# High and low value parts from one matmul of 129 columns, in the last 24 of 32 attention pairs

## The chip, the cores and the metric

The kernel runs on one core of a Trainium2 chip. The metric is the device time of one execution in microseconds. Engines are named as in the profile: PE multiplies matrices, PEld is its weight load, DVE is the vector engine, ACT the scalar engine, POOL the GpSimd engine, SP issues DMA transfers. Before the change the kernel took 1162.68 us (median of three runs, 1161.75 to 1164.28).

## The reference

Attention over pooled queries, and behind it a gated unit over the attention's output. What the change touches is the last product of the attention, `attn @ v`, and its division by the row sums:

```python
def _attn_ref(q, k, v):                       # 8 batches, 8 heads, 1152 keys, 64 dims
    q_pool = q.reshape(B, H, S // 2, 2, D).mean(axis=3)          # 576 queries
    scores = scale * np.matmul(q_pool, k.transpose(0, 1, 3, 2))
    scores = scores - np.max(scores, axis=-1, keepdims=True)
    attn = np.exp(scores)
    attn = attn / (np.sum(attn, axis=-1, keepdims=True) + 1e-09)
    return np.matmul(attn, v)

def _moe_ref(x, w_in, w_spatial, b_spatial, w_out):              # x: attention output, 8 x 576 x 512
    h = np.maximum(x @ w_in, 0.0)
    u, v = h[..., :512], h[..., 512:]
    v_n = (v - mean(v)) / np.sqrt(var(v) + 1e-06)
    v_s = np.einsum('ts,bsd->btd', w_spatial, v_n) + b_spatial[None, :, None]
    return (u * v_s) @ w_out
```

## The kernel before

The 64 heads are worked in 32 pairs (`i` from 0 to 31). Every fp32 factor is held as two 16-bit parts, a high one and a low one, and a product is the sum of the matmuls of its parts. For a pair, `attention(i)` goes through 18 steps, nine key chunks of 128 for each of the two heads. A step makes a 128x512 tile of transposed scores in a bank `pss` (two matmuls, L1081 and L1082), ACT writes its exponential to the tile `pt` (L1087), and POOL takes the rest of `pt` apart in place (L1107): `top` is the upper half of each fp32 word read as bf16, `rst` the remainder as fp16. The last 64 queries of a head are worked apart, in `ptl` and `tail_values` (L1051 to L1053).

Two steps later `values(i, k)` multiplies the step's `pt` with the chunk's values. The values lie in `vp` as 130 columns a chunk: 0 to 63 the low part, 64 to 127 the high part, 128 a column of ones, 129 unused. The 512 queries are four blocks of 128, and each block has 65 columns in the bank `o`: 64 of output, and one that collects the row sums from the ones. A step has twelve matmuls in three rounds over the four blocks: `top` with high part and ones (65 columns, L977), `top` with the low part onto the first 64 of the same columns (L983), `rst` with high part and ones (65 columns, L988). In the first eight pairs (`i < EARLY`) three of the nine chunks go through whole fp32 matmuls instead (L970).

There is one bank `o` (`ps_o` with one buffer). It is full after a head's ninth chunk. Then DVE adds a small constant to the four row sums and takes the reciprocal (L949 and L950, `den`) and multiplies the four blocks into the tile `xm` (L996), and the next head's first matmul may write the bank. `turn()` puts off a head's first value step by one step more, so that other work lies between two heads. After a pair's second head `xm` is turned over, from the ninth pair on through ACT, POOL and a transposing DMA (L1006, L1007).

Beside these steps run, as generators advanced at set rates: `maxima` of the next pair (matmuls L869 and L854 of 384 columns into `pm`, DVE maxima L875), `prep` of the pair after that, the values of the next pair, and from the ninth pair on the gated unit of the two batches that are finished (L1168, L1235, L1279, L1280, L1322, with `vv<-u,gs,vv` at L496 on DVE).

The order on the engines isn't the order of the code. `Order.pin` collects all instructions with their dependencies, gives each a cost by size and engine, goes twice through a list schedule (forward, then a backward pass that ranks by time to the end, then forward again), and pins the order that comes out on every engine. A different instruction, or another cost, can so change the order of everything after it.

Of the kernel before, what the change touches and what calls it, by code (L numbers as in the profile page):

```python
# [17 lines left out]
AF = mybir.ActivationFunctionType  # L18
ALU = mybir.AluOpType
# [356 lines left out]
def attn_sgu_kernel(ctx: ExitStack, tc: tile.TileContext, qT, kT, v, w_in, w_spT, b_sp, w_out, out):  # L376
    nc = tc.nc
    P = 128
    B, NHP, _, D, _, S = qT.shape
    NC = kT.shape[4]  # L380
# [17 lines left out]
    WHOLE = (1, 4, 7)  # L398
    EARLY = 2 * NHP
    MOE_RATE = 0.5  # L400
    D1 = D + 1
    VW = 2 * D + 2
# [262 lines left out]
    whole = {}  # L665
# [280 lines left out]
    def inverse(src, name):  # L946

        r = sm.tile(list(src.shape), F32, name=name, bufs=2)
        nc.vector.tensor_scalar_add(r, src, 1e-9 * PEXP)  # L949
        nc.vector.reciprocal(r, r)  # L950
        return r
# [4 lines left out]
    def values(i, k):  # L956


        st = state[i]
        h, c = divmod(k, NC)  # L960
        if c == 0:
            st["o"] = ps_o.tile([P, MAIN], F32, name="o")
        o = st["o"][:, : 4 * D1].rearrange("p (t d) -> p t d", d=D1)
        pt = st["pt"][k]
        top = pt.bitcast(BF16)[:, 1::2]
        rst = pt.bitcast(F16)[:, 0::2]
        vp = vps[i % 2][:, h, c]
        if i < EARLY and c in WHOLE:
            for t in range(4):
                nc.tensor.matmul(  # L970
                    o[:, t], lhsT=pt[:, t * P : (t + 1) * P], rhs=whole[i][:, h, WHOLE.index(c)],
                    start=False, stop=False, skip_group_check=True,
                )
            return
        for t in range(4):
            cols = slice(t * P, (t + 1) * P)
            nc.tensor.matmul(  # L977
                o[:, t], lhsT=top[:, cols], rhs=vp[:, D : D + D1], start=c == 0 and t == 0, stop=False,
                skip_group_check=True,
            )  # L980
        for t in range(4):
            cols = slice(t * P, (t + 1) * P)
            nc.tensor.matmul(  # L983
                o[:, t, 0:D], lhsT=top[:, cols], rhs=vp[:, 0:D], start=False, stop=False, skip_group_check=True
            )
        for t in range(4):
            cols = slice(t * P, (t + 1) * P)
            nc.tensor.matmul(  # L988
                o[:, t], lhsT=rst[:, cols], rhs=vp[:, D : D + D1], start=False, stop=c == NC - 1,
                skip_group_check=True,  # L990
            )
        if c == NC - 1:
            if h == 0:
                st["xm"] = wk.tile([P, 4, P], F32, name="xm", bufs=1)
            r = inverse(o[:, :, D], "den")
            nc.vector.tensor_tensor(  # L996
                out=st["xm"][:, :, h * D : (h + 1) * D], in0=o[:, :, 0:D],
                in1=r.unsqueeze(2).to_broadcast([P, 4, D]), op=ALU.mult,
            )
            if h == 1:  # L1000
                later.append([2, lambda: turn_main(i)])
# [12 lines left out]
    def turn_main(i):  # L1014

        b, hp = divmod(i, NHP)
        n, e = divmod(b, 2)
        xm = state.pop(i)["xm"]
        if i < EARLY:
            ps = ps_m.tile([P, 512], F32, name="pm")  # L1020
            for t in range(4):
                nc.tensor.transpose(out=ps[:, t * P : (t + 1) * P], in_=xm[:, t], identity=ident)
            x_split(x_rows(n, e)[:, :, hp], ps)
        else:
            turn_by_dma(xm, n, e, hp)
        if hp == NHP - 1:
            xc = wk.tile([P, 2, NHP, P], F16, name="xc", bufs=1)
            nc.scalar.activation(xc[:, 0], xt, AF.Copy, bias=0.0, scale=1.0)
            nc.gpsimd.tensor_sub(xc[:, 1], xt, xc[:, 0])
            ps = ps_m.tile([P, 512], F32, name="pm")  # L1030
            for k in range(2 * NHP):
                nc.tensor.matmul(
                    ps[:, k * TAIL : (k + 1) * TAIL], lhsT=xc[:, k // NHP, k % NHP], rhs=ident2, start=True, stop=True
                )
            nc.scalar.activation(
                x_rows(n, None)[:, :, :, e * TAIL : (e + 1) * TAIL],
                ps.rearrange("p (l k t) -> p l k t", l=2, t=TAIL), AF.Copy, bias=0.0, scale=1.0,
            )
            if ends_unit(i):
                units.append(gated_unit(n))  # L1040
# [18 lines left out]
    def turn(last=False):  # L1059

        while todo and (last or len(todo) > LAG):
            if not last and todo[0][1] % NC == 0 and len(todo) <= LAG + 1:
                break
            values(*todo.popleft())
        for x in list(later):
            x[0] -= 1
            if x[0] <= 0 or last:
                later.remove(x)
                x[1]()
# [420 lines left out]
```

## Time and profile before

| | |
|---|---|
| timed runs | 1162.68 us median (1161.75 to 1164.28) |
| profiled execution | a span of 1164.0 us from first to last instruction; it has no time of its own beside the runs |
| granted TensorE clock | 0.996 on average |
| instructions in the profile | 33534 |
| matmuls | 13297, each with a weight load |
| value matmuls at L977, L983, L988 | 2112 each, 193 ns mean length of one |
| DMA | 133.18 MB in 89146 packets |

The page is read by asking first which engine is short of time, then in which stage. A matmul's length (193 ns here) is from its start until its result has landed; the next one starts long before that, so what a matmul takes of PE is the distance from its start to the next start. The profile shows two stages with attention: the first eight pairs, up to about 250 us, with loads, weights and little else for PE to turn to, and the remaining 24 pairs together with the gated units, up to about 1064 us. Behind them comes the last gated unit alone.

```profile
PE   4989999999999999999999999999999999999998
DVE  7799999977889987865778757874778757742644
ACT  6788889997879978778877878878787876844433
POOL 3667766888998988879887888978878888974000
```

These are the busy tenths in 40 slices of 29.1 us: PE is at 9 from the third slice on, while the three others keep some room.

### The profile page before, as it was taken

The page shows a single profiled execution, that of the slowest core. Times are in us where ns is not written, and L with a number is a line of the kernel's source. Part 1 is how long each engine was busy: PE and PEld are TensorE (multiplying, and loading weights), DVE is VectorE, ACT ScalarE, POOL GpSimd, SP SyncE. Part 2 cuts the span into 40 slices and gives each one's busy share as a digit, 9 for nine tenths or more (in the row PEclk, how much of TensorE's full clock was granted, in tenths as well). Part 3 has the DMA queues.
Part 4 walks back from the last instruction along what each step waited for, and adds up shares of the span by engine and source line. Part 5 has one row for each costly group of instructions (what it writes and reads, how often), then busy time and mean ns, then how long its engine had stood idle before and what let it go on. Part 6 is the DMA issues. An engine that isn't in the chain of part 4 may idle for free.

```text
span 1164.0 us, 33534 instructions
## 1 busy us (share of the span) xinstructions
PE 1131.7 (97%) x13297; PEld 718.2 (62%) x13297; DVE 870.9 (75%) x2239; ACT 892.4 (77%) x1697; POOL 860.6 (74%) x739
## 2 busy tenths in 40 slices
PE   4989999999999999999999999999999999999998
PEld 1667777766666665665666666566666666665453
DVE  7799999977889987865778757874778757742644
ACT  6788889997879978778877878878787876844433
POOL 3667766888998988879887888978878888974000
PEclk9989999999999999999999999999999999999999
DMA  6666455444553354454433444355533412221002
GB/s 208 185 206 168 131 167 179 122 123 123 137 144 83 77 139 109 142 143 125 125 96 83 145 120 110 99 133 159 144 92 99 128 34 68 47 63 37 1 1 82
DMA packets 89146, 133.18 MB, mean 114 GB/s; under 512 B 39902, under 2 KB 48158, under 8 KB 88988
## 3 DMA queue, kind: packets, MB, share of 16 engines
q1 hardware_dynamic: 88988, 131.04, 40.4%
q8 instruction: 104, 1.70, 0.6%
q14 instruction: 54, 0.44, 0.1%
HBM read 81.20 MB, written 9.44 MB: 78 GB/s over the span
## 4 chain that ended last, share of the span: by engine, by line
PE 85%; DVE 8%; ACT 3%; DMA 2%; issue 1%; SPq 0%; POOL 0%; ACTq 0%; DVEq 0%; POOLq 0%
PE pss L1081 9%; PE pss L1082 9%; PE pm L869 8%; PE pw L1279 7%; PE pw L1235 6%; PE pw L1168 6%; PE pw L1322 6%; PE o L977 5%; PE o L988 5%; PE o L983 5%; DVE mt L875 3%; PE o L970 3%; PE pm L1051 1%; PE pss L1168 1%; PE pm L1053 1%; PE pm L1052 1%
## 5 line engine op out<-in xcount | busy, mean ns | idle before, releaser
L1107 POOL TENSOR_TENSOR pt<-pt 128x512 f16<-128x512 f32 x528 | 579.0, 1115 | 154.1 <-ACT pt L1087 149.7
L1087 ACT ACTIVATE pt<-pss,esc 128x512 f32<-128x512 f32 x576 | 388.6, 693 | 130.0 <-PE pss L1082 115.0
L875 DVE TENSOR_REDUCE mt<-pm 128x1 f32<-128x384 f32 x733 | 385.7, 551 | 104.8 <-PE pm L869 94.2
L1081 PE MATMUL pss<-qhi,khi 128*128 128x512 f16 x576 | 219.5, 382 | 2.3 <-ACT pt L1087 2.1
L1082 PE MATMUL pss<-xq,klo 66*128 66x512 f16 (+1 forms) x576 | 219.7, 383 | 0.8 <-DMA xq<-mr 0.8
L869 PE MATMUL pm<-khi,qhi 128*128 128x384 f16 x637 | 194.0, 327 | 3.7 <-DVE mt L875 3.3
L977 PEld LDWEIGHTS <-pt 128*128 128x128 bf16 x2112 | 123.4, 98 | 60.3 <-issue 3.3
L977 PE MATMUL o<-vp,pt 128*128 128x65 f16 x2112 | 158.7, 193 | 0.3 <-DVE xm L996 0.2
L983 PE MATMUL o<-vp,pt 128*128 128x64 f16 x2112 | 157.0, 193 | 0.0
L988 PE MATMUL o<-vp,pt 128*128 128x65 f16 x2112 | 156.7, 193 | 0.0
L988 PEld LDWEIGHTS <-pt 128*128 128x128 f16 x2112 | 115.2, 98 | 36.5 <-issue 1.6
L869 PEld LDWEIGHTS <-qhi 128*128 128x128 f16 x756 | 72.9, 100 | 63.0 <-issue 11.8
L983 PEld LDWEIGHTS <-pt 128*128 128x128 bf16 x2112 | 103.6, 98 | 5.5 <-issue 0.3
L1168 PE MATMUL pw<-wi_h,xg 128*128 128x512 f16 x240 | 88.4, 379 | 0.5 <-ACT row L1342 0.5
L1235 PE MATMUL pw<-xg,wi_h 128*128 128x512 f16 (+1 forms) x336 | 82.1, 325 | 0.0
L1322 PE MATMUL pw<-wo_h,vv 128*128 128x512 f16 x216 | 78.6, 380 | 2.3 <-DVE vv L496 2.3
L1279 PE MATMUL pw<-ws_h,vv 128*128 128x512 f16 x216 | 78.2, 379 | 0.2 <-DVE u L1289 0.2
L1107 POOL TENSOR_TENSOR ptl<-ptl 128x1152 f16<-128x1152 f32 x32 | 69.8, 2181 | 9.7 <-ACT ptl L1103 9.5
L875 DVE TENSOR_REDUCE mt<-pw 128x1 f32<-128x384 f32 x131 | 69.4, 545 | 9.8 <-PE pw L869 5.1
L1103 ACT ACTIVATE ptl<-pss,esc 128x256 f32<-128x256 f32 (+1 forms) x128 | 64.6, 505 | 10.7 <-PE pss L1098 10.3
L1082 PEld LDWEIGHTS <-klo 66*128 66x128 f16 (+1 forms) x576 | 56.4, 98 | 26.0 <-issue 4.7
L1081 PEld LDWEIGHTS <-khi 128*128 128x128 f16 x576 | 56.7, 99 | 22.7 <-issue 2.6
(270 smaller groups left out, 2530.5 us busy)
## 6 DMA issues: line engine op xcount, KB each, us to landing
vt<-in_v_dram SPq DMA_DIRECT2D x56, 576.0 KB
qt<-in_qT_dram SPq DMA_DIRECT2D x32, 576.0 KB
kt<-in_kT_dram SPq DMA_DIRECT2D x32, 576.0 KB
khi<-kn SPq DMA_DIRECT2D x128, 144.0 KB
out_dram<-row SPq DMA_DIRECT2D x24, 256.0 KB
qhi<-xq SPq DMA_DIRECT2D x62, 72.0 KB
klo<-klo SPq DMA_DIRECT2D x31, 144.0 KB
u<-in_w_in_dram SPq DMA_DIRECT2D x3, 1024.0 KB
```

The source lines that it names most:

```text
L869: nc.tensor.matmul(pm[:, :W], lhsT=q[:, c0 : c0 + P], rhs=k[:, n * NB : (n + 1) * NB, :], start=True, stop=True,)
L875: nc.vector.reduce_max(out=mt[:, t, n : n + 1], in_=pm[:, :W], axis=AX.X)
L977: nc.tensor.matmul(o[:, t], lhsT=top[:, cols], rhs=vp[:, D : D + D1], start=c == 0 and t == 0, stop=False, skip_group_check=True,)
L983: nc.tensor.matmul(o[:, t, 0:D], lhsT=top[:, cols], rhs=vp[:, 0:D], start=False, stop=False, skip_group_check=True)
L988: nc.tensor.matmul(o[:, t], lhsT=rst[:, cols], rhs=vp[:, D : D + D1], start=False, stop=c == NC - 1, skip_group_check=True,)
L1081: nc.tensor.matmul(o, lhsT=khh[:, h, c, :], rhs=qhl[:, h, q], start=True, stop=False)
L1082: nc.tensor.matmul(o, lhsT=KL[0:rows, h, c, :], rhs=X[0:rows, h, q], start=False, stop=True)
L1087: nc.scalar.activation(pt, ps, AF.Exp, bias=0.0, scale=esc)
L1107: nc.gpsimd.tensor_sub(t.bitcast(F16)[..., 0::2], t, t.bitcast(BF16)[..., 1::2])
L1168: nc.tensor.matmul(ph, lhsT=rows(xa, cc, c0, c0 + P), rhs=wa[:, cc, DH:DF], start=n == 0, stop=n == 3 * NCC - 1,)
L1235: nc.tensor.matmul(pu[:, : z - a], lhsT=wa[:, cc, fc * P : (fc + 1) * P], rhs=rows(xa, cc, a, z), start=n == 0, stop=n == 3 * NCC - 1,)
L1279: nc.tensor.matmul(pv, lhsT=l, rhs=r[:, 0:MAIN], **fl)
```

## The change

From the ninth pair on (`joint = i >= EARLY`) the blocks stand 130 columns apart in the bank `o` (`pitch = VW`) in place of 65. For blocks 1 to 3, `top` is multiplied with low part, high part and ones in one matmul of 129 columns: the low part's product lands in the 64 columns ahead of the block, the rest in the block. Block 0 keeps two matmuls. The products of `rst` stay as they were. A step has nine matmuls in place of twelve, in an order written out. At the head's end ACT copies the three low products out of the bank into `xm` (L1007 of the changed kernel), DVE adds this copy to the three blocks in the bank (L1010), and then multiplies as before (L1011). The first eight pairs keep their twelve matmuls.

```diff
+        bank = st["o"]
+        joint = i >= EARLY
+        pitch = VW if joint else D1
+        def at(a, n, z=D):
+            return bass.AP(bank.tensor, bank.offset + a, [list(bank.ap[0]), [pitch, n], [1, z]])
...
+        hi, lo = slice(D, D + D1), slice(0, D)
+        def product(x, t, v, a, z):
+            nc.tensor.matmul(
+                bank[:, t * pitch + a : t * pitch + z], lhsT=x[:, part[t]], rhs=v,
+                start=c == 0 and t == 0 and x is top and z == D1, stop=x is rst and c == NC - 1, skip_group_check=True,
+            )
...
-        for t in range(4):
-            cols = slice(t * P, (t + 1) * P)
-            nc.tensor.matmul(o[:, t], lhsT=top[:, cols], rhs=vp[:, D : D + D1], ...)
-        for t in range(4):
-            cols = slice(t * P, (t + 1) * P)
-            nc.tensor.matmul(o[:, t, 0:D], lhsT=top[:, cols], rhs=vp[:, 0:D], ...)
-        for t in range(4):
-            cols = slice(t * P, (t + 1) * P)
-            nc.tensor.matmul(o[:, t], lhsT=rst[:, cols], rhs=vp[:, D : D + D1], ...)
+        if joint:
+            product(top, 0, vp[:, hi], 0, D1)
+            for t in range(1, 4):
+                product(top, t, vp[:, 0 : D + D1], -D, D1)
+            product(rst, 1, vp[:, hi], 0, D1)
+            product(rst, 2, vp[:, hi], 0, D1)
+            product(top, 0, vp[:, lo], 0, D)
+            product(rst, 3, vp[:, hi], 0, D1)
+            product(rst, 0, vp[:, hi], 0, D1)
+        else:
+            for x, v, z in ((top, hi, D1), (top, lo, D), (rst, hi, D1)):
+                for t in range(4):
+                    product(x, t, vp[:, v], 0, z)
         if c == NC - 1:
...
-            r = inverse(o[:, :, D], "den")
+            x = st["xm"][:, :, h * D : (h + 1) * D]
+            if joint:
+                nc.scalar.activation(x[:, 1:4], at(VW - D, 3), AF.Copy, bias=0.0, scale=1.0)
+            r = inverse(at(D, 4, 1)[:, :, 0], "den")
+            if joint:
+                nc.vector.tensor_add(at(VW, 3), at(VW, 3), x[:, 1:4])
             nc.vector.tensor_tensor(
-                out=st["xm"][:, :, h * D : (h + 1) * D], in0=o[:, :, 0:D],
-                in1=r.unsqueeze(2).to_broadcast([P, 4, D]), op=ALU.mult,
+                out=x, in0=at(0, 4), in1=r.unsqueeze(2).to_broadcast([P, 4, D]), op=ALU.mult
             )
```

On PE the order is the same up to the first value step of the ninth pair. There, in the middle of the step, stands before (`vp_101` is the values tile, `pt` the exponentials, the number at the end the output's columns):

```order
L977 MATMUL o<-vp_101,pt 128x65
L983 LDWEIGHTS pt
L983 MATMUL o<-vp_101,pt 128x64
L983 LDWEIGHTS pt
L983 MATMUL o<-vp_101,pt 128x64
```

And now, from the step's first joint matmul but two on:

```order
L980 MATMUL o<-vp_101,pt 128x129
L980 LDWEIGHTS pt
L980 MATMUL o<-vp_101,pt 128x65
L980 LDWEIGHTS pt
L980 MATMUL o<-vp_101,pt 128x65
L980 LDWEIGHTS pt
L980 MATMUL o<-vp_101,pt 128x64
```

Twelve loads and twelve matmuls became nine and nine; over the kernel PE has 1,296 loads and 1,296 matmuls fewer.

The second place is DVE at the end of the second head of pair 13, where the gated unit of the first two batches stands before its last product. Before:

```order
L949 TENSOR_SCALAR den<-o 128x4
L875 TENSOR_REDUCE mt<-pm 128x1 x2
L950 RECIPROCAL den<-den 128x4
L875 TENSOR_REDUCE mt<-pm 128x1
L996 TENSOR_TENSOR xm<-o,den 128x4x64
L888 TENSOR_REDUCE pm<-mt 128x4
```

And now:

```order
L949 TENSOR_SCALAR den<-o 128x4
L1071 TENSOR_SCALAR xt<-pm,dent 64x64 x2
L950 RECIPROCAL den<-den 128x4
L1010 TENSOR_TENSOR o<-o,xm 128x3x64
L1011 TENSOR_TENSOR xm<-o,den 128x4x64
L875 TENSOR_REDUCE mt<-pm 128x1 x5
```

The add stands ahead of the multiply, and the maxima that stood between moved behind both.

The third place is ACT at the same head's end. Before:

```order
L710 ACTIVATE vp_102<-vt 128x9x64
L1087 ACTIVATE pt<-pss,esc 128x512 x2
L1103 ACTIVATE ptl<-pss,esc 128x5x64
L1087 ACTIVATE pt<-pss,esc 128x512
L1103 ACTIVATE ptl<-pss,esc 128x5x64
```

And now:

```order
L709 ACTIVATE vt<-vt,vs 128x576 x2
L710 ACTIVATE vp_102<-vt 128x9x64
L1007 ACTIVATE xm<-o 128x3x64
L710 ACTIVATE vp_102<-vt 128x9x64
L1101 ACTIVATE pt<-pss,esc 128x512 x2
```

The copy stands between two parts of the next pair's values, and the exponentials of the next steps stand behind it.

More of the change, by code (lines that the diff above doesn't have):

```diff
@@ L962, in values @@
             st["o"] = ps_o.tile([P, MAIN], F32, name="o")
-        o = st["o"][:, : 4 * D1].rearrange("p (t d) -> p t d", d=D1)
+        bank = st["o"]
[3 more added lines that the diff above has]
+            return bass.AP(bank.tensor, bank.offset + a, [list(bank.ap[0]), [pitch, n], [1, z]])
         pt = st["pt"][k]
@@ L967, in values @@
         vp = vps[i % 2][:, h, c]
-        if i < EARLY and c in WHOLE:
+        part = [slice(t * P, (t + 1) * P) for t in range(4)]
+        hi, lo = slice(D, D + D1), slice(0, D)
[4 more added lines that the diff above has]
+            )
+        if not joint and c in WHOLE:
             for t in range(4):
[L970 to L973, printed above, removed]
+                product(pt, t, whole[i][:, h, WHOLE.index(c)], 0, D1)
             return
-        for t in range(4):
-            cols = slice(t * P, (t + 1) * P)
[L977 to L980, printed above, removed]
-        for t in range(4):
-            cols = slice(t * P, (t + 1) * P)
-            nc.tensor.matmul(
-                o[:, t, 0:D], lhsT=top[:, cols], rhs=vp[:, 0:D], start=False, stop=False, skip_group_check=True
-            )
-        for t in range(4):
-            cols = slice(t * P, (t + 1) * P)
[L988 to L991, printed above, removed]
+        if joint:
[11 more added lines that the diff above has]
+                    product(x, t, vp[:, v], 0, z)
         if c == NC - 1:
```

## The prediction

> **What bounds the kernel now.** I read the busy shares first, then the chain that ended last, then busy time by stage, then what PE waited for once the first pairs were through.
>
> ```profile
> PE 1131.7 (97%) x13297; PEld 718.2 (62%) x13297; DVE 870.9 (75%) x2239; ACT 892.4 (77%) x1697; POOL 860.6 (74%) x739
> ...
> PE 85%; DVE 8%; ACT 3%; DMA 2%; issue 1%; SPq 0%; POOL 0%; ACTq 0%; DVEq 0%; POOLq 0%
> ```
>
> ```profile
> 250.00:1064.00 814.00, 808.29 (x10029) 509.03 (x10025) 596.69 (x1561) 639.98 (x1215) 689.62 (x593) 1.00 0.40 108
> 1064.00:1164.00 100.00, 96.19 (x587) 46.73 (x585) 49.79 (x118) 37.69 (x72) 2.31 (x2) 1.00 0.09 28
> ```
>
> ```profile
> PE pw L1322 <- DVE vv L496: 2.3, 1, 2.3
> PE pm L869 <- DVE mt L875: 1.2, 3, 0.5
> ...
> PE o L977 <- DVE xm L996: 0.2, 1, 0.2
> ```
>
> PE carries 85% of the chain. The columns of the second fence are the stretch, its length, then PE, PEld, DVE, ACT and POOL: between 250 and 1064 us, where the changed pairs run, PE is busy for 808.29 of 814 us, the others for 597 to 690. Busy PE could still hide slack, since matmuls overlap, so I also took the distances between matmul starts (below): they are as short as the columns allow nearly everywhere, and the third fence, PE's waits from 250 us on, holds little more than 5 us. In this stage a nanosecond off PE's stream is a nanosecond off the end, until another engine gives out; the fullest of the others is POOL with 690 of 814, and the change gives POOL nothing.
>
> **What a value step costs PE.** The longest unbroken stretch of value matmuls, four steps:
>
> ```profile
> 308.84 0.28 PE L977 MATMUL o<-vp,pt 128*128 128x65 f16 x4
> 308.96 0.28 PE L983 MATMUL o<-vp,pt 128*128 128x64 f16 x4
> ...
> 310.28 0.38 PE L1081 MATMUL pss<-qhi,khi 128*128 128x512 f16 x1
> ```
>
> ```profile
> 308.80:310.29 1.49, 1.45 (x48) 0.00 (x0) 0.00 (x0) 1.00 1.01 331
> ```
>
> 48 matmuls start from 308.84 to 310.28: 1.44 / 48 = 30.0 ns each, for 64.7 columns on average. No matmul of 129 columns is in this trace, but the tail's values have 130, 128 and 130:
>
> ```profile
> 300.95 0.22 PE L1051 MATMUL pm<-vp,ptl 128*128 128x130 f16 x1
> 301.01 0.22 PE L1052 MATMUL pm<-vp,ptl 128*128 128x128 f16 x1
> ...
> 302.50 0.32 PE L869 MATMUL pm<-khi,qhi 128*128 128x384 f16 x1
> ```
>
> ```profile
> L1051 PE MATMUL pm<-vp,ptl x9: 218/218/221, 300.9 to 302.3; 128*128 128x130 f16 x9
> L1052 PE MATMUL pm<-vp,ptl x9: 217/218/219, 301.0 to 302.4; 128*128 128x128 f16 x9
> L1053 PE MATMUL pm<-vp,ptl x9: 218/219/220, 301.1 to 302.4; 128*128 128x130 f16 x9
> ```
>
> 27 of them in 302.50 − 300.95 = 1.55 us: 57.4 ns each for 129.3 columns. The two points give (57.4 − 30.0) / (129.3 − 64.7) = 0.424 ns a column and a constant of 30.0 − 64.7 × 0.424 = 2.6 ns a matmul.
>
> **Removed.** The step streams as many columns as before (4 × 65 + 4 × 64 + 4 × 65 = 776; after, 3 × 129 + 64 + 5 × 65 = 776). What goes is three matmuls of twelve, each with its weight load: three constants, 7.8 ns. With 24 pairs × 18 steps = 432 steps, that is 1,296 matmuls and 1,296 × 2.6 = **3.4 us off PE**. The bounds: were a joint matmul as slow as the two it replaces, nothing; were it at the bare column rate (129 × 0.424 = 54.7 against 60.0), 1,296 × 5.3 = 6.9 us. I take the value of the tail's rows, the nearest in size and form. A loss here would need an exposed weight load:
>
> ```profile
> L977 PEld LDWEIGHTS <-pt 128*128 128x128 bf16 x2112 | 123.4, 98 | 60.3 <-issue 3.3
> ```
>
> A load lasts 98 ns and there was one for each of the 48 and of the 27, at 30.0 and 57.4 ns, so loads overlap and set neither pace. Nor will the new order in a step, in which a block is written again after two other matmuls where it was four: the tail's three write the same columns in direct succession.
>
> **Added.** At each of 48 head ends ACT copies 128x192 from the bank into xm, and DVE adds that copy back onto the bank. Neither form is in the trace.
>
> ```profile
> L1103 ACT ACTIVATE ptl<-pss,esc 128x256 f32<-128x256 f32 (+1 forms) x128 | 64.6, 505 | 10.7 <-PE pss L1098 10.3
> ```
>
> ```profile
> L1245 ACT ACTIVATE u<-pw,r_h 128x64 f32<-128x64 f32 x28 | 7.5, 327 | 0.0
> ```
>
> ```profile
> L996 DVE TENSOR_TENSOR xm<-o,den 128x256 f32<-128x256 f32 x64 | 26.8, 419 | 1.7
> L1289 DVE TENSOR_TENSOR u<-u,pw 128x64 f32<-128x64 f32 x27 | 5.8, 214 | 0.0
> ```
>
> The ACT group of 505 ns mixes 256 and 320 columns, 288 on average. Copy: between 327 (64) and 505 (288), on the line at 192, 0.43 us. Add: between 214 (64) and 419 (256), 0.35 us. That is 48 × 0.43 = 21 us more for ACT (640 becomes 661 of 814, 81%) and 48 × 0.35 = 17 us for DVE (597 becomes 614, 75%). Both lie beside PE's stream and cost nothing there by themselves; without that cover all 48 × 0.78 = 37 us would show.
>
> **Moved: the head end's chain.** There is one bank o, so the next head's first value matmul waits for the multiply. How that goes now, at one of the thinnest places:
>
> ```profile
> 729.62 0.29 PE L988 MATMUL o<-vp,pt 128*128 128x65 f16 x4
> ...
> 729.94 0.16 DVE L949 TENSOR_SCALAR den<-o 128x4 f32<-128x4 f32 x1
> ...
> 730.86 0.41 DVE L996 TENSOR_TENSOR xm<-o,den 128x256 f32<-128x256 f32 x1
> ...
> 731.33 0.18 PEld L977 LDWEIGHTS <-pt 128*128 128x128 bf16 x4 [0.62 <-DVE xm L996]
> ```
>
> The last value matmul ends at 729.91, the multiply at 731.27, the next head starts at 731.33; PE's stream stood for 0.3 us. The chain becomes: copy (0.43), add (0.35), multiply (0.42), with about 0.1 us at each of two passings between engines and 0.2 us of the last matmul's own length, 1.6 us from its start; denominator and reciprocal fall beside the copy. Behind the copy wait ACT's next exponentials, behind the add DVE's maxima, so each is late by that much, and ACT may first have to end what it is in: up to 0.69 us. The need is 1.6 to 2.3 us. Against it I counted the matmuls that stand in PE's new order between the two heads, at 216 ns for 512 columns, 163 for 384, 57 for 130 and 30 for the small ones: 3.6 us on average over the 48 (3.1 before). The thinnest are pair 13's second head (1.3 us; 2.3 before), pair 21's second head (1.7; 1.3 before), and four between 2.0 and 2.2. New stalls: about 0.6, 0.3, and none to 0.2 at the four, together 0.9 us. Heads that waited before (0.3 us at 731, and 0.3 and 0.2 in two others by the start distances) now have 1.7, 2.2 and 3.1 us between, so some 0.6 us of old stalls goes. Net **+0.3 us**, with ends −0.8 and +3 (all six short by ACT's wait).
>
> The last 100 us, from 1064 on, come after the last head and keep their order; up to the first joint matmul, at about 250 us, all engines keep theirs.
>
> **Sum.** 1164.0 us of span − 3.4 + 0.3 = 1160.9. The profiled execution lies in the timed runs (1161.75 to 1164.28), 1.3 us over their median; what lies around the span drops out, as I carry only the difference: 1162.7 − 3.1 = **1159.6 us**. From 0.2% (2.3 us) on the runs can tell a change from none: faster means below 1160.4, slower above 1165.0.
>
> **Rivals.** *The bank's chain becomes the bound (slower).* If ACT runs more than 1.5 us behind at a usual head end, 3.6 us between heads no longer do; 0.4 us short at 20 of the 48 is 8 us: 1162.7 − 3.4 + 8 = 1167.3. For it: ACT is the engine that gets the most work, and its queue is in order. Against it: the average cover exceeds the need by over 1 us, and ACT has 150 us free in this stage. It decides once the mean shortfall over all heads passes (3.4 + 2.3) / 48 = 0.12 us. 10%.
>
> *A held DVE operation comes or goes.* One row of the stage stands out:
>
> ```profile
> 457.63 3.81 DVE L496 SCALAR_TENSOR_TENSOR vv<-u,gs,vv 128x576 f16<-128x576 f32 x1
> ```
>
> ```profile
> 453.73 5.03 POOL L1107 TENSOR_TENSOR pt<-pt 128x512 f16<-128x512 f32 x5
> 458.71 2.11 POOL L1107 TENSOR_TENSOR ptl<-ptl 128x1152 f16<-128x1152 f32 x1
> ```
>
> ```profile
> 461.50 0.60 PE L1322 MATMUL pw<-wo_h,vv 128*128 128x512 f16 x2 [2.31 <-DVE vv L496]
> ...
> 462.44 0.52 PE L869 MATMUL pm<-khi,qhi 128*128 128x384 f16 x1
> ```
>
> Its like take 1.28 us on average; this one took 3.81 while POOL ran without a gap, PE stood for 2.3 us, and then ran some matmuls slowly (0.52 for 0.33), worth another 1.7 to 1.9 us by the start distances. That is 4.2 us from one chance meeting. The new order keeps that operation at the same place, behind a head end whose operations moved. If it is spared: 1159.6 − 4.2 = 1155.4, 12%. If another is hit elsewhere, in 800 us of new order: 1163.8, 11%.
>
> *Even starts speed the whole step.* Before, blocks start at multiples of 65 columns, after at even ones. The score tails start at multiples of 64:
>
> ```profile
> 528.72 0.28 PE L1094 MATMUL pss<-qhi,khi 128*128 128x64 f16 x4
> 528.83 0.28 PE L1098 MATMUL pss<-xq,klo 66*128 66x64 f16 x4
> 528.95 0.38 PE L1168 MATMUL pw<-wi_h,xg 128*128 128x512 f16 x1
> ```
>
> Eight in 0.23 us are 28.8 ns for 64 columns, so 29.1 for the 64.7 columns of a value matmul, which now takes 30.0: up to 0.9 ns for each of nine matmuls in 432 steps, 3.5 us: 1156.1, 14%. [...]
>
> *Wide pairs run slower.* Were a load-and-matmul pair bound by its load at these widths, each joint matmul would take up to the load's 98 ns, 38 more than the two it replaces: 1,296 × 38 = 49 us, 1212. The 27 pairs at 57.4 ns speak against it: 1%. [...]
>
> *The joint matmul saves nothing*: 1162.7 + 0.3 = 1163.0, 2%.
>
> **How the numbers follow.** My forecast gets 50%, with 1157.5 to 1161.5 as its own range. Faster: three quarters of it, and the two rivals below it, 62%. Slower: most of the chain's rival, a second held operation, the slow pairs: 12%. The same: 26%. The range reaches to the spared operation below and the second meeting above: 1154.6 to 1164.0.
>
> **What would show it.** Right: 1,296 fewer matmuls; value steps of nine in about 350 ns where twelve took 360; PE's busy share unchanged at 97%; the copy at 0.43, the add at 0.35 us; PE's waits for xm under 1.5 us in all. Wrong: steps that still take 360 or more; starts of the first value matmul put down to xm at many heads; long DVE operations beside an unbroken POOL, with slow matmuls behind them.

## The result and the profile after

The changed kernel is slower: 1175.83 us in the median of six runs (1173.52 to 1177.39) beside 1164.26 us (1161.75 to 1166.11) for the kernel before, a ratio of 1.0095 with a 95% interval of [1.0083, 1.0108] (the medians' own quotient is 1.0099). The forecast was 1159.6, and the range ended at 1164.0.

First the busy shares and the chain that ended last of the profiled execution after (1176.99 us, span 1175.2):

```profile
PE 1131.5 (96%) x12001; PEld 713.0 (61%) x12001; DVE 879.5 (75%) x2287; ACT 904.9 (77%) x1745; POOL 858.9 (73%) x739
...
PE 77%; DVE 10%; ACT 7%; DMA 2%; issue 2%; POOL 1%; SPq 0%; ACTq 0%; DVEq 0%; POOLq 0%
```

PE has its 1,296 matmuls fewer, but the chain now runs through PE for 77% where it was 85%, and through DVE and ACT for 17% where it was 11%. The stages, with the same columns as before (stretch, its length, PE, PEld, DVE, ACT, POOL):

```profile
250.00:1076.00 826.00, 807.65 (x8705) 504.32 (x8702) 607.00 (x1608) 651.17 (x1260) 686.13 (x591) 1.00 0.40 106
1076.00:1176.00 100.00, 95.44 (x584) 46.32 (x582) 49.76 (x118) 37.72 (x72) 2.31 (x2) 0.99 0.08 27
```

The last gated unit takes 100 us as before. The stage of the changed pairs went from 814 to 826 us, while PE is busy in it for no longer (807.65 after 808.29): PE stood still. What it stood for is in PE's waits from 250 us on (what waited, what it waited for, us in all, how often, the longest):

```profile
PE pm L897 <- DVE wide L893: 4.1, 5, 1.2
PE pm L869 <- DVE mt L875: 3.3, 8, 0.8
PE pm L869 <- DVE mr L899: 2.9, 4, 1.1
PE pm L869 <- DVE xt L1071: 1.6, 2, 1.0
PE pw L1336 <- DVE vv L496: 1.3, 1, 1.3
...
PE o L980 <- DVE xm L1011: 0.4, 1, 0.4
```

The view's rows sum to 17.0 us where they summed to 5.2 before. Only 0.4 us are waits for the bank `o`. 13.3 us are waits for DVE's work on the next pair: shift, maxima, tails. Why DVE was late is in its own waits, of the kernel after and of the kernel before:

```profile
DVE den L949 <- ACT xm L1007: 42.9, 35, 11.5
```

```profile
DVE den L949 <- PE o L988: 16.8, 13, 11.9
```

Each kernel has one long wait (11.5 and 11.9 us), at the very last head, where DVE has nothing else to do. Without it the row sums waited 12 times for PE before, 4.9 us in all; now they wait 34 times for ACT's copy, 31.4 us in all. One such place in the timeline of after (start, length, engine, line, operation, and in brackets the wait ahead of it):

```profile
350.13 1.17 ACT L490 ACTIVATE klo<-kt 128x1152 f16<-128x1152 f32 x1
...
351.28 0.52 ACT L1259 ACTIVATE u<-pw,r_h 128x64 f32<-128x64 f32 x2
...
351.67 0.55 ACT L1117 ACTIVATE ptl<-pss,esc 128x320 f32<-128x320 f32 x1
...
352.08 0.36 ACT L1007 ACTIVATE xm<-o 128x192 f32<-128x192 f32 x1
...
352.47 0.16 DVE L949 TENSOR_SCALAR den<-o 128x4 f32<-128x4 f32 x1 [1.95 <-ACT xm L1007]
352.67 0.18 DVE L950 RECIPROCAL den<-den 128x4 f32<-128x4 f32 x1
352.78 0.28 DVE L899 CAST mr<-pm 8x128 f16<-8x128 f32 x1
...
353.11 0.32 PE L869 MATMUL pm<-khi,qhi 128*128 128x384 f16 x1 [1.09 <-DVE mr L899]
```

The head's last value matmul ended at 350.42. The copy is queued on ACT behind other work and ends at 352.44. DVE has come to the row sums 1.95 us before they start and stands. Behind them in its queue is the cast of the shift (`mr`), which the next matmul of the maxima waits for, and so PE stands for 1.09 us.

The row sums and the copy only read the bank, at different columns. Still the built program makes the one wait for the other. Each of the 48 row-sum instructions of the late pairs waits on ACT's counter; in the kernel before, 47 of them wait on PE's. One of each:

```
before  L949 TENSOR_SCALAR den<-o 128x4 [waits PE_49]
after   L949 TENSOR_SCALAR den<-o 128x4 [waits Activation_49]
```

The copy stands ahead of the row sums in the code, and the built program orders the two engines on the bank although both only read it; in the kernel that copies on DVE (below) none of the 48 row sums waits on ACT. Every kernel here with the copy on ACT keeps the two apart, so what they would do without the wait isn't shown. The kernel's own planner doesn't know this wait: `Order.edges` links two accesses only if one of them writes. It planned the row sums for the moment when PE ends the head, and pinned them there in DVE's queue.

### The profile page after: what moved, and what is told of

The parts are those of the page before. It is cut to its first block, busy times and chain, and to the rows that moved or that the text cites. A ratio compares the mean times of both kernels' runs of the same rounds, so it can differ in the third digit from the quotient of the medians.

```text
span 1175.2 us, 31071 instructions
## 1 busy us (share of the span) xinstructions
PE 1131.5 (96%) x12001; PEld 713.0 (61%) x12001; DVE 879.5 (75%) x2287; ACT 904.9 (77%) x1745; POOL 858.9 (73%) x739
## 4 chain that ended last, share of the span: by engine, by line
PE 77%; DVE 10%; ACT 7%; DMA 2%; issue 2%; POOL 1%; SPq 0%; ACTq 0%; DVEq 0%; POOLq 0%
PE o L980 16%; PE pss L1096 8%; PE pss L1095 8%; PE pm L869 7%; PE pw L1293 6%; PE pw L1249 6%; PE pw L1336 6%; PE pw L1182 5%; DVE mt L875 4%; ACT pt L1101 2%; PE pss L1182 1%; PE pss L1293 1%; PE pm L1065 1%; PE pm L1067 1%; PE pm L1066 1%
## 5 line engine op out<-in xcount | busy, mean ns | idle before, releaser
L980 PEld LDWEIGHTS <-pt 128*128 128x128 bf16 (+1 forms) x5040 | 259.0, 98 | 106.2 <-issue 5.5
L980 PE MATMUL o<-vp,pt 128*128 128x65 f16 (+2 forms) x5040 | 302.3, 200 | 0.4 <-DVE xm L1011 0.4
L869 PE MATMUL pm<-khi,qhi 128*128 128x384 f16 x637 | 194.1, 326 | 9.6 <-DVE mt L875 4.2
L869 PEld LDWEIGHTS <-qhi 128*128 128x128 f16 x756 | 72.8, 100 | 63.1 <-issue 11.3
L1336 PE MATMUL pw<-wo_h,vv 128*128 128x512 f16 x216 | 77.3, 379 | 1.3 <-DVE vv L496 1.3
L712 POOL TENSOR_TENSOR vp<-vt,vp 128x576 f16<-128x576 f32 x48 | 60.1, 1252 | 20.4 <-ACT vp L710 18.9
L826 POOL TENSOR_TENSOR klo<-kt,kn 128x640 f16<-128x640 f32 (+1 forms) x48 | 65.0, 1357 | 6.8 <-ACT kn L825 6.8
L1182 PEld LDWEIGHTS <-xg 128*128 128x128 f16 x432 | 40.1, 97 | 40.4 <-issue 1.5
L1293 PEld LDWEIGHTS <-vv 128*128 128x128 f16 x384 | 37.1, 98 | 35.5 <-issue 0.8
```

Of the source, the lines that this page charges most:

```text
L826: nc.gpsimd.tensor_sub(KL[:, 0, a:z], k0[:, a:z], kn[:, a:z])
L869: nc.tensor.matmul(pm[:, :W], lhsT=q[:, c0 : c0 + P], rhs=k[:, n * NB : (n + 1) * NB, :], start=True, stop=True,)
L980: nc.tensor.matmul(bank[:, t * pitch + a : t * pitch + z], lhsT=x[:, part[t]], rhs=v, start=c == 0 and t == 0 and x is top and z == D1, st ...
L1182: nc.tensor.matmul(ph, lhsT=rows(xa, cc, c0, c0 + P), rhs=wa[:, cc, DH:DF], start=n == 0, stop=n == 3 * NCC - 1,)
L1293: nc.tensor.matmul(pv, lhsT=l, rhs=r[:, 0:MAIN], **fl)
L1336: nc.tensor.matmul(py, lhsT=ga[:, fc, c0 : c0 + P], rhs=wa[:, fc, :], start=m == 0, stop=m == end - 1)
```

## The experiments

The theory: PE is slowed by this unplanned wait. Its rivals: the copy and add themselves (work on ACT and DVE, a longer chain), the joint matmuls, chance meetings of DVE with POOL, and chance in the order that the planner arrives at. In the expectations these are W (the wait), L (the load of copy and add), J (the joint matmul), H (DVE operations held while POOL runs) and R (another order as such). Ratios are to the kernel before in its own order, on the same chip. PE's standing time is worked out from the distances between matmul starts, from 251 us to the last value matmul: what a distance exceeds the median of its size by, where that is over 60 ns.

**The planner told of the wait.** The wait stays in the program, but the order is now made with it.

```diff
-                        if m != n and (write or w):
+                        if m != n and (write or w or (a[0][0] == "o" and prog[m].engine != ins.engine)):
```

> Theory W (the wait): the row-sum step on DVE waits for ACT's copy, because both read bank o; the scheduler does not know of this wait, so DVE stands with other work behind it. Here the scheduler alone is told of it (one condition in its dependency pass, for tile o). W expects 1160 to 1165 us, DVE's wait for the copy down from 42.9 us to under 12, PE's stalls of over 60 ns in the changed pairs down from 28 to about 11 us. Theory L (the load): the copy and the add themselves crowd ACT and DVE; the work is the same here, so L expects 1173 to 1177. Theory R (reshuffle): any new order in these pairs costs some 10 us by where it puts things; R expects 1168 to 1180, with stalls at other places.

Measured: 1164.41 us (1159.56 to 1169.68, 12 runs), ratio 1.0012 [0.9993, 1.0031]. The waits of DVE in its profile, a run of 1161.86 us:

```profile
DVE den L949 <- ACT xm L1007: 16.1, 9, 11.5
```

Without the long one, 8 waits of 4.6 us in all are left of 34 with 31.4, and the ratio falls by 0.83%, some 10 us. The twelve runs lie in two groups, 1159.6 to 1161.9 and 1167.0 to 1169.7, six in each. PE's standing time in this run is 10.9 us, against 27.8 in the change and 10.4 before. So the wait has the main share, but without it the change brings no measurable gain in this order.

**The row sums last.** The copy and the add come ahead of the row sums, so that DVE has only one place to wait.

```diff
-            r = inverse(at(D, 4, 1)[:, :, 0], "den")
             if joint:
                 nc.vector.tensor_add(at(VW, 3), at(VW, 3), x[:, 1:4])
+            r = inverse(at(D, 4, 1)[:, :, 0], "den")
```

> The row-sum step is emitted behind the add, so the wait for the copy moves to the add, for which the scheduler already plans it. W expects 1160 to 1166 us (a chain longer by 0.3 us at each head end, most of it beside PE work) and the row-sum step no longer waiting for ACT. L expects 1173 to 1177, since the work is the same. R expects 1168 to 1180.

Measured: 1171.62 us (1167.83 to 1173.45, 6 runs), 1.0064 [1.0047, 1.008]: 4 us back, less than half of what was expected. The wait for the copy is now the add's (20.4 us in 9 waits, one of them 11.3), so the unplanned waits are gone here too. Behind the copy stand the same four DVE operations as in the change, in another order. What keeps this kernel slow is in part another thing: in its profile one DVE operation (`vv`, L496) is held for 5.50 us, and PE waits 3.7 us for `vv`. The rest of its loss isn't traced.

**The copy on DVE.** Then no other engine reads the bank at the head's end.

```diff
-                nc.scalar.activation(x[:, 1:4], at(VW - D, 3), AF.Copy, bias=0.0, scale=1.0)
+                nc.vector.tensor_copy(out=x[:, 1:4], in_=at(VW - D, 3))
```

> The copy goes to DVE, ahead of the row sums: no wait between engines is left, but DVE gets some 16 us of work more and ACT as much less. W expects 1161 to 1167 us. L, where it is DVE's load that counts, expects 1177 to 1185; where it is ACT's, about 1165. R expects 1168 to 1180.

Measured: 1168.48 us (1168.01 to 1170.39, 5 runs), 1.005 [1.0038, 1.0062]. 5 us come back and 6 remain, though no such wait is left; W expected 1167 at most. In its profile one operation on DVE (`vv`, L496) takes 4.59 us where its like took 1.28 before, and PE's standing time ahead of the matmuls that read `vv` (L1336) is 5.6 us, so this order has a loss of its own.

**No copy and no add.** The low parts' products of three blocks of four are left out of the output; the joint matmuls stay.

```diff
-            if joint:
-                nc.scalar.activation(x[:, 1:4], at(VW - D, 3), AF.Copy, bias=0.0, scale=1.0)
             r = inverse(at(D, 4, 1)[:, :, 0], "den")
-            if joint:
-                nc.vector.tensor_add(at(VW, 3), at(VW, 3), x[:, 1:4])
```

> The copy and the add are left out, so the low parts of three query blocks of four are missing from the output; the joint matmuls stay. W and L both expect 1158 to 1162 us, PE's 3.4 to 4 us less and no new stalls. R expects 1168 to 1180.

Measured: 1165.40 us (1163.26 to 1167.75, 11 runs), 1.002 [1.0011, 1.0028]: slower than expected by 3 us or more. Its timeline has the cause of most of it:

```profile
452.27 4.05 POOL L1117 TENSOR_TENSOR pt<-pt 128x512 f16<-128x512 f32 x4
455.04 8.07 DVE L496 SCALAR_TENSOR_TENSOR vv<-u,gs,vv 128x576 f16<-128x576 f32 x1 [0.46 <-ACT vv L493]
456.26 1.17 POOL L1017 TENSOR_TENSOR xc<-xm,xc 128x512 f16<-128x512 f32 x1
457.38 2.12 POOL L1117 TENSOR_TENSOR ptl<-ptl 128x1152 f16<-128x1152 f32 x1
459.44 3.05 POOL L1117 TENSOR_TENSOR pt<-pt 128x512 f16<-128x512 f32 x3
```

One DVE operation takes 8.07 us. It starts within a run of POOL instructions without a gap, of which nine are shown, and ends 0.6 us behind the last of them. PE's longest wait for it is 6.4 us:

```profile
PE pw L1332 <- DVE vv L496: 7.2, 2, 6.4
```

It is the held operation of the prediction, at twice its length. What the joint matmuls save can't be read off this kernel's time.

**Twelve matmuls, with copy and add.** The low products go one by one into their own columns, and the head's end is that of the change.

```diff
-            product(top, 0, vp[:, hi], 0, D1)
-            for t in range(1, 4):
-                product(top, t, vp[:, 0 : D + D1], -D, D1)
...
+            for t in range(4):
+                product(top, t, vp[:, hi], 0, D1)
+            for t in range(4):
+                product(top, t, vp[:, lo], -D if t else 0, 0 if t else D)
+            for t in range(4):
+                product(rst, t, vp[:, hi], 0, D1)
```

> Twelve matmuls a step as before, but the low products go to columns of their own, and the copy and the add stand at the head's end as in the change (with the wait that the scheduler does not know). The head's end alone, without the joint matmul. W expects the change's loss and none of its gain: 1175 to 1180 us, DVE's wait for the copy about 43 us. A theory that the joint matmul itself costs the time (J) expects 1162 to 1166.

Measured: 1172.35 us (1169.7 to 1173.34, 5 runs), 1.0065 [1.0044, 1.0087]. The new head's end alone, with 34 waits for the copy (35.8 us with one of 11.3), costs 7.5 us: less than in W's 1175 to 1180, and too much for a theory that puts the whole loss on the joint matmuls. The change itself is slower still by 0.3%, with its shorter stream (standing time 27.8 us, here 19.8), though the two intervals just overlap; the kernels have different orders, and this difference is not traced.

**The starts of the blocks alone.** This is the kernel before, its four blocks 130 columns apart, with the same order.

```diff
-        o = st["o"][:, : 4 * D1].rearrange("p (t d) -> p t d", d=D1)
+        o = st["o"][:, : 3 * VW + D1]
+        o = bass.AP(o.tensor, o.offset, [list(o.ap[0]), [VW, 4], [1, D1]])
```

> The kernel before with its four blocks 130 columns apart in place of 65 and nothing else: the order on every engine stays the same, and every block starts at an even column. The rival on even starts expects 1159 to 1160 us and matmul starts 0.5 to 0.9 ns closer in value steps; without it 1162 to 1164 and no change in the distances.

Measured: 1162.72 us (1160.12 to 1165.85, 12 runs), 0.9987 [0.9975, 0.9999]. The stretch of 48 value matmuls that the prediction used, in this kernel:

```profile
306.87 0.28 PE L978 MATMUL o<-vp,pt 128*128 128x65 f16 x4
...
308.30 0.38 PE L1082 MATMUL pss<-qhi,khi 128*128 128x512 f16 x1
```

1.43 / 48 = 29.8 ns a matmul, before 30.0, read to 0.01 us. Over all distances between neighbouring value matmuls behind 251 us, some 4,600 in each kernel (one of 70 ns before is left out), the means are 30.03 and 30.14 ns. Over the 5,184 of the late pairs that is 0.6 us, not 3.5; by the time it is 1.5 us, with an interval from 0.1 to 2.9.

**Work moved off DVE.** The split of `u` goes to ACT and POOL, once with the planned wait, once in the kernel before.

```diff
-                    head(gt[0][:, fc, r], u[:, fc, r], s_g)
-                    rest(gt[1][:, fc, r], u[:, fc, r], s_g, gt[0][:, fc, r])
+                    nc.scalar.activation(u[:, fc, r], u[:, fc, r], AF.Copy, bias=0.0, scale=s_g)
+                    nc.scalar.activation(gt[0][:, fc, r], u[:, fc, r], AF.Copy, bias=0.0, scale=1.0)
+                    nc.gpsimd.tensor_sub(gt[1][:, fc, r], u[:, fc, r], gt[0][:, fc, r])
```

> e1 (scheduler told of the wait) whose runs fell in two groups, 1159.6 to 1161.9 and 1167 to 1169.7. Here the rest of the gated values, which DVE was caught with while POOL ran without a gap (vv<-u,gs,vv), is made by POOL itself after a scaling on ACT. Theory H (holds by POOL make the two groups) expects one group, no DVE operation over 2.4 us, and 1158 to 1163 us; if POOL's 31 us more cost time, both this and e9 are later by the same. Without H: two groups again, 7 us apart.

> The kernel before with the same move of that rest to POOL. H expects 1158 to 1163 us (the 3.8 us operation and PE's slow stretch behind it gone, up to 4 us, less what POOL's 31 us more cost); e8 below it by the 3.4 to 4 us of the joint matmul. If order alone decides, the two differ by anything from -8 to +8.

Measured: 1167.85 us (1166.83 to 1170.09, 9 runs), 1.0032 [1.0019, 1.0046], and 1164.18 us (1163.47 to 1166.9, 12 runs), 1.0007 [0.9994, 1.0019]. No gain in either, and both lie above what H expected, the first by 5 us. The first has one group of runs, as H expected, but at the place of the upper group of the change with the planned wait. The operation that was held is gone, but another split on DVE (`qhi`, L496) takes 3.13 us in its profile, POOL is busy for 707 us from 250 to 1064 us, and PE's standing time is 19.3 us. So this move doesn't show that held operations make the two groups.

**Other orders.** All of these kernels also differ by where chance puts their operations. So the same four stages of the change were run in two more orders, which a larger slack in the planner gives: in the first for DVE's work that PE waits for, in the second for ACT's. The kernel before keeps its order on all four engines up to about 320 us in both.

```diff
+                more = 100 if (e, lane[m]) == ("DVE", "PE") and m > 0.3 * size else 0
-                due[m] = max(due[m], x + (self.SLACK.get((e, lane[m]), 0) if through else 0))
+                due[m] = max(due[m], x + (self.SLACK.get((e, lane[m]), 0) + more if through else 0))
```

In the second order it says "Activation" for "DVE". Besides this edit each kernel is the one before, the change, the change with the planned wait, or the change without copy and add (where the same low parts are missing).

> The kernel before, with one slack of the scheduler (results of DVE awaited by PE) raised by 100 ns for the last 70% of the instructions: the same work in another order from about 350 us on. If a chance order costs as such (theory R: the order before was the best of many), 1164 to 1172 us and PE's stalls over 10.5 us; without R 1161 to 1165.

> The change with the same other order. W expects it above the same order of e1 (p1_edge) by 6 to 12 us, with DVE's wait for the copy over 35 us here.

> The change with the wait told to the scheduler (as e1) and the same other order. Joint matmul and no unplanned wait: 1159 to 1168 us by where POOL catches DVE's operations; by W under p1_after, by the stream's 3.6 us under p1_before when neither is caught.

> The joint matmuls without the copy and the add (the low parts of three query blocks of four are missing from the output), in the first other order. Theory C (what is left of the loss once the wait is planned is the head end's longer chain) expects 1156 to 1159 us, 3 to 4 below p1_before, PE's stalls under 10 us. Theory R (order alone makes the rest) expects 1159 to 1167 here as in e4, with stalls of 11 to 17 us and no link to the head's end.

> The kernel before with another slack raised (results of ACT awaited by PE, by 100 ns, the last 70%): a second other order. R expects 1164 to 1172 us, without R 1161 to 1165.

> The change in the second other order. W expects 1173 to 1180 us, DVE's wait for the copy over 35 us, 8 to 14 us over p2_edge.

> The change with the wait told to the scheduler, in the second other order: 1160 to 1168 us; the value matmuls 3.6 us shorter in all than in p2_before.

> The same in the second other order. C expects 1160 to 1163 us, 3 to 5 below p2_before; R anything from 1158 to 1168.

Measured, as medians and ratios:

| | its own order | first other order | second other order |
|---|---|---|---|
| before | 1 | 1160.87, 0.9976 [0.9967, 0.9985] | 1165.52, 1.0011 [0.9997, 1.0026] |
| joint, no copy and add | 1165.40, 1.002 [1.0011, 1.0028] | 1156.67, 0.9931 [0.9914, 0.9948] | 1168.27, 1.0021 [1.0002, 1.004] |
| change, wait planned | 1164.41, 1.0012 [0.9993, 1.0031] | 1164.12, 0.9998 [0.9984, 1.0013] | 1171.8, 1.0042 [1.0022, 1.0062] |
| change | 1175.83, 1.0095 [1.0083, 1.0108] | 1178.08, 1.0119 [1.0097, 1.0142] | 1174.42, 1.0076 [1.0059, 1.0093] |

The last step, the unplanned wait, has the same sign in all three: 0.83%, 1.21% and 0.34%, or 10, 14 and 4 us. The 14 is over the 6 to 12 that W expected there, the 4 under the 8 to 14. In the second order the intervals of the two kernels overlap: of the ten runs of the change with the planned wait, eight lie between 1171.1 and 1174.4, two at 1163.6 and 1165.2, and why isn't shown. Three more expectations missed. The kernel before in the second order lies half a us above the 1161 to 1165 that it should have kept without R. With the wait planned, the change in the first order should have been 3.6 us faster than the kernel before there; it is 3 us slower. And the joint matmuls alone in the second order, expected at 1160 to 1163, took 1168.27. DVE's waits for the copy in the first order, with the wait unplanned and planned:

```profile
DVE den L950 <- ACT xm L1008: 40.7, 34, 11.5
```

```profile
DVE den L950 <- ACT xm L1008: 18.4, 8, 11.5
```

The first other order is the only one in which no profile, of the four kernels, has a DVE operation over 2.4 us, so its steps can be read best: the joint matmuls bring 0.45% (5 us), copy and add with the planned wait take 0.67% (8 us), the unplanned wait another 1.21% (14 us). In the two other orders the joint matmuls alone are 0.2% and 0.1% slower than the kernel before in the same order, with held operations of 8.07 us in one and of 6.88 and 4.04 in the other. The stage from 250 us on, before (first) and with the joint matmuls alone:

```profile
250.00:1059.00 809.00, 805.23 (x10002) 507.66 (x9998) 591.98 (x1559) 638.25 (x1212) 691.57 (x591) 1.00 0.41 108
```

```profile
250.00:1054.00 804.00, 799.95 (x8696) 503.10 (x8695) 593.48 (x1558) 638.40 (x1212) 687.42 (x591) 1.00 0.41 108
```

PE is busy for 5.3 us less, and the last value matmul starts 4.3 us sooner (the stretches are set to whole us); DVE and ACT have the same work as before. The first line's kernel is the fastest of those that compute the whole output, and it doesn't have the change.

Held operations may also make the two groups of runs. The second order's joint matmuls alone have three runs at 1161.9 to 1163.9 and seven at 1167.2 to 1171.0. The profiled run, of 1167.8 us, has this:

```profile
1000.87 6.88 DVE L497 SCALAR_TENSOR_TENSOR vv<-u,gs,vv 128x576 f16<-128x576 f32 x1
...
1000.90 1.17 POOL L1018 TENSOR_TENSOR xc<-xm,xc 128x512 f16<-128x512 f32 x1
...
1004.08 3.05 POOL L1118 TENSOR_TENSOR pt<-pt 128x512 f16<-128x512 f32 x3
```

PE waits 7.6 us for `vv` there. The profiles from a lower group, of the change with the planned wait in its own order and in the second one, have no DVE operation over 2.6 us. But no kernel was profiled in both of its groups, so the cause of the groups stays open.

**What is left with the wait planned.** Two kernels in the first order ask why copy and add cost 8 us. In one, DVE multiplies high and low products apart and POOL adds them in SBUF; in the other the copy is on DVE, as above.

```diff
-                nc.scalar.activation(x[:, 1:4], at(VW - D, 3), AF.Copy, bias=0.0, scale=1.0)
...
-                nc.vector.tensor_add(at(VW, 3), at(VW, 3), x[:, 1:4])
...
+                nc.vector.tensor_tensor(
+                    out=y, in0=at(VW - D, 3), in1=r[:, 1:4].unsqueeze(2).to_broadcast([P, 3, D]), op=ALU.mult
+                )
+                nc.gpsimd.tensor_add(x[:, 1:4], x[:, 1:4], y)
```

> The joint matmul in the first other order, with the head's end without ACT: DVE multiplies high and low products by the reciprocal one after the other, which frees the bank, and POOL adds the two in SBUF. If what p1_edge loses to p1_no_add (7.4 us) is the chain through ACT and back, 1157 to 1160 us, under p1_before (1160.9) and so under both kernels of the change; if it is any work at the head's end, or POOL's 27 us more, 1161 to 1168.

> The change with the copy on DVE, in the first other order. If the loss left in p1_edge is the passing between ACT and DVE, 1157 to 1161 us; if it is the longer chain ahead of the next head or DVE's work, 1163 to 1168.

Measured: 1168.22 us (1166.9 to 1169.88, 5 runs), 1.0042 [1.0028, 1.0055], with POOL busy for 714 of 814 us; and 1163.67 us (1162.72 to 1165.96, 10 runs), 1.0002 [0.9992, 1.0013], the same as with the copy on ACT and the wait planned. The first time is at the upper end of what was expected for work at the head's end. The second says that most of the 8 us isn't the passing from ACT to DVE. Up to 3 us of it could hide here: that is PE's standing time ahead of the matmuls that read `vv` (L1337), one of which waited for a DVE operation of 2.71 us. The unplanned wait is gone from this kernel without any edit to the planner, and with it 14 us against the change in the same order. Whether the 8 us are DVE's added work or the longer hold on the bank isn't settled: no kernel had the one without the other.

## Why the prediction was wrong

**The step that failed** is "the head end's chain", in the words "denominator and reciprocal fall beside the copy", and with it the net of +0.3 us. They do not fall beside it: the row sums wait for it, 34 times with 0.9 us on average, and DVE's work for the next pair stands behind them, at no price in the sum. The wait stands in the built program's instructions and needs no run to be seen; the prediction worked with the order of the operations and with what reads and writes what. Planning the wait takes 4 to 14 us back in three orders.

**The rest of that step was mis-sized too.** With the wait planned, copy and add cost 8 us against the joint matmuls alone. The prediction named the work behind the add ("DVE's maxima, so each is late by that much") but priced only what holds the next head's first value matmul. In the first order PE's standing time is 7.2 us without copy and add, 15.1 with them and the wait planned (a run 2 us over its median), 26.0 unplanned; before the change it is 7.7. Divided over 48 heads, 8 us are 0.16 us a head, small beside the 3.6 us of cover that the prediction counted: cover for the bank, not for the maxima. The other two orders go the same way: without copy and add PE's standing time is 15.5 and 18.9 us, but 9.5 and 9.1 of it stand before the matmuls that read the held `vv`, which leaves 6.0 and 9.8; with them and the wait planned it is 10.9 and 14.1, in runs of the lower groups. And ACT was taken to be at most 0.69 us late with the copy. It started more than that after the head's last value matmul had ended at 10 of the 48 heads, 1.73 us at the latest; the kernel before already had operations of 1.16 us (`klo`, L490) in this stage, and in the timeline above `klo`, `u` and `ptl` stand ahead of the copy.

**Right: what bounds the kernel.** From 251 us to the last value matmul, PE's standing time rose from 10.4 us to 27.8, of which 13.1 before L869 and 5.3 before L897, and the stretch grew by 11.5 us. The failed step lies in the condition attached to it, "until another engine gives out": DVE gave out by its order, not by its load (607 of 826 us).

**Right: the stream.** Four steps after the change, in the timeline:

```profile
1035.07 1.57 PE L980 MATMUL o<-vp,pt 128*128 128x65 f16 x36
...
1036.47 0.38 PE L1336 MATMUL pw<-wo_l,vv 128*128 128x512 f16 x1
```

36 matmuls from 1035.07 to 1036.47 are 1.40 / 4 = 350 ns a step, as forecast. The same stretch without its standing time is 795.9 to 799.3 us in the fourteen joint kernels, 797.3 on average, and 799.4 to 802.1 in the six with twelve matmuls, 800.5 on average: 3.2 us for the 3.4 of the sum. Single kernels scatter by over 1 us about these means; the kernel before and the change alone, 802.1 and 796.1, would give 6.0.

**Right: copy and add.** From the groups of after (busy us, mean ns, idle time before):

```profile
L1007 ACT ACTIVATE xm<-o 128x192 f32<-128x192 f32 x48 | 15.8, 330 | 7.5 <-PE o L980 6.9 <-POOL pt L1121 0.5
L1010 DVE TENSOR_TENSOR o<-o,xm 128x192 f32<-128x192 f32 x48 | 16.9, 352 | 0.4
```

0.33 and 0.35 us, for 0.43 and 0.35.

**The rivals.** That the bank's chain becomes the bound had the right sign and nearly the right mechanism, ACT late with the copy, but the wrong place: PE waits 0.4 us for the bank and stands before the maxima. The held operation of 3.81 us is gone after the change (its longest DVE operation of that kind takes 2.74 us), which the loss hides; in other kernels operations of this kind were held for 3 to 8 us. Even starts are worth 0.6 us by the distances and 1.5 by the time, with an interval from 0.1 to 2.9, which leaves the 3.5 out. Slow wide pairs are refuted: a load and a matmul took 39 ns on average over widths of 64 to 129. That the joint matmul saves nothing is refuted by the stream and by the first other order. The chances don't add up in one place: the rows named for "faster" give 63.5%, not 62, and the second held operation, counted as slower, is priced at 1163.8, which the forecast's own bounds call the same.

**The checks named in advance.** PE's waits for `xm` stayed under 1.5 us, as the forecast wanted, while 11 us were lost. The check looked only at the wait that the prediction had in mind; the sum of all of PE's waits (5.2 to 17.0 us) would have shown it at once.

## What to carry to other kernels

Where an operation on a second engine joins a bank that another engine reads, take the waits from the built program, not from what reads and writes what: with an order pinned by a planner, give the planner the same waits, or an engine stands, as DVE here for 31.4 us in 34 waits, with everything behind it. Price an operation on a side engine by what stands behind it in that engine's queue, also where the resource that it holds has time to spare. And where a planner makes the order, try a change of half a per cent in several orders: here the kernel before alone ranged from 0.9976 to 1.0011 without any change to its work.

## What the hardware showed

The DVE operation `vv<-u,gs,vv` took 1.28 us on average before, but once 3.81 us, and 8.07 and 6.88 us in the two timelines above, each time beside a run of POOL instructions without a gap. In each of the two timelines at least five POOL instructions ran from start to end while it lasted. Sixteen such operations in the twenty profiles took over 2.6 us, and each ended 0.61 to 0.62 us behind the end of a POOL instruction. For twelve of them, among these all ten of over 2.8 us, POOL then paused for 53 ns or more; the other four, of 2.66 to 2.74 us, ended while POOL went on without a gap. That POOL's work holds them is the author's reading of these times; how it would do so isn't shown.
